# Attention, routed experts and an MLP in one kernel: routing the last batch in two groups, and moving weight loads, splits and slot loads around the first expert passes

## The chip, the cores and the metric

One core of a Trainium2 chip runs the whole program. The metric is device microseconds of one execution, lower is better. Engines are named as in the profile: PE (TensorE), DVE (VectorE), ACT (ScalarE), POOL (GpSimd), SP (SyncE, which here only issues DMAs; its queue is shown as SPq).

## What is computed

```python
# q, k, v: (4, 8, 576, 64)   s: (4, 8, 576)
scores = scale * q @ k.T                                   # causal
scores += min(-(cum[:, None] - cum[None, :]), 0)           # cum = cumsum(max(s, 0))
x = softmax(scores) @ v            # as 2304 tokens x 512
e = argmax(x @ w_gate, axis=1)     # 8 experts, one for each token
g = softmax(x @ w_gate)[e]
y[t] = g[t] * relu(x[t] @ w1[e]) @ w2[e]                   # w1 512x1024, w2 1024x512
h = y @ w_in                                               # 512x2048, float64 in DRAM
out = (h * clip(h + 3, 0, 6) / 6) @ w_out                  # 2048x512, float64 in DRAM
```

## The kernel before

**Precision.** Every product is taken with numbers split in two 16-bit halves, "hi" and "lo", and three matmuls stand for one. So each weight has to be loaded in float32 (64 pieces `wf` of 512 KB) and split. `piece` (lines 215 to 243) returns a job in two steps: `ld` takes a staging tile and issues the load on SP, `sp` splits it. With `act=True` the split is one ACT instruction (line 234) and one DVE instruction (line 237); with `act=2` it is POOL (229), ACT (230) and POOL (231).

**Attention.** A unit is 128 query rows (the fifth of a batch has 64) of one of the four batches: 20 units of 4 head pairs each, so N = 80 pairs. Line 973 walks the pairs; `todo` holds work for given slots n (`at_slot`), and `at_time` turns a time, counted with the prices of line 862, into a slot. The last two units are taken in the order 19, 18 (line 71).

**Routing.** For a finished unit `rows_out` scales the rows (ACT 639, POOL 640) and writes them to DRAM, `logits` transposes them by DMA and returns the gate's matmuls as `mm`. `route` (14 DVE instructions and one of ACT) picks the experts of a group of units, `place_tokens` ranks the tokens with small matmuls and scatters them into the slot table `tok_d` with one indirect DMA of POOL for each unit (line 739). `counts` (line 752) works out the tables of all passes after the last group; its result `dyn_i` is read by SP into registers. Before the change a batch is one group. Units 17, 19 and 18 are finished too late for the attention loop: their `mm`, then `route`, `place_tokens` and `counts` of the fourth batch, are hooks that run behind the blocks f = 0, 1, 2 and 4 of the first expert pass.

**Expert passes.** There are ten passes over `CAP_A`, 128 or `CAPS` rows. Passes 0 and 1 take 224 rows each of experts 0 and 1, and only tokens of the first three batches; passes 2 and 3 take what is left of those two experts (128 rows); passes 4 to 9 take the other six, sorted by load. A pass p has eight blocks `expert_hidden` (f = 0..7, 12 matmuls, ReLU on ACT line 1046, lo half on DVE line 1047) and four output blocks (d = 0..3, 24 matmuls at line 1151, then lines 1157 to 1159). All share five PSUM buffers (pool `pb`). `load_slots` reads the slots of a pass (line 193), `load_x` gathers its rows by an indirect DMA of POOL (line 200) and transposes them by DMA on SP (line 204); both stand behind the hidden blocks of the pass two before. `feed(x)`, called behind block f as x = f and behind block d as x = 8 + d, issues loads and splits of coming weights; `load` orders each load behind a marked transpose with `tc.issue_after`, and `split` can be told (`early`) not to wait for `mark["pos"]`.

**What sets the order.** The program text gives priorities; a scheduler with a simulated timeline then puts each engine's instructions in the order in which it takes them to be ready. On the chip every engine and the SP queue keep that order, whatever is late. An instruction that was written later can so stand in front of one written earlier.

**Weights before the change.** In attention, `w_load` takes four pieces of w1 and four of w2 of expert 0 and three of w1 of expert 1, at slots 52, 54 .. 72, each split three slots later; the staging tiles are the two buffers "q32" of the attention's own loads. The five pieces left of expert 1 are loaded in pass 0 at x = 0..4, behind `mark["x0"]`, the transpose of unit 17, and split at x = 5..9. Pass 1 loads four of expert p4, pass 2 loads four more and splits four at its output blocks, pass 3 splits four.

Of the kernel before, what the change touches and what calls it, by code (L numbers as in the profile page):

```python
# [8 lines left out]
F32 = mybir.dt.float32  # L9
F16 = mybir.dt.float16  # L10
BF16 = mybir.dt.bfloat16
I32 = mybir.dt.int32
# [15 lines left out]

LATE = 5


@with_exitstack
def kernel(
# [160 lines left out]

    def load_x(p):

        t = (rings["odd"] if p % 2 else rt).tile([128, 2 * KD, (CAP + 15) // 16 * 16], F16, tag="xsT", name="xsT", bufs=1)
        for x, (a, m) in enumerate(blocks((passes[p] + 15) // 16 * 16)):
            xg = row_tile([128, 2 * DM], F16, "xg")
            mark["pool"] = nc.gpsimd.indirect_dma_start(  # L200
                out=xg[:m], out_offset=None, in_=x_d[:min(col0[u] for u in late) if p < NS else NT, :],
                in_offset=Offset(ap=slots[:m, p, x, 0:1], axis=0),
            ).ins
            mark["xs", p] = nc.sync.dma_start_transpose(out=t[:, :, a:a + m], in_=xg[:m]).ins
        return t


# [9 lines left out]
    def piece(src, halves, sc, view, act=False):  # L217
# [3 lines left out]
        def ld():  # L221
            f = stage[0].tile([128, 1024], F32, tag=stage[1], name="wf")
            fv = view(f)
# [60 lines left out]
    with ExitStack() as at:  # L284
        ac = at.enter_context(tc.tile_pool(name="ac", bufs=1))
        a2 = at.enter_context(tc.tile_pool(name="a2", bufs=2))
        a3 = at.enter_context(tc.tile_pool(name="a3", bufs=3))
        stage.update({0: a2, 1: "q32"})
        psS = at.enter_context(tc.tile_pool(name="psS", bufs=3, space=PSUM))
# [359 lines left out]
        def logits(u, g):  # L649
# [13 lines left out]

            if place[u] == NU - 3:
                mark["x0"] = mark["x"]

            def half(t, c):
# [245 lines left out]
        for b in range(B):  # L913
            us = [u for u in range(NU) if units[u][0] == b]
            groups += [us] if b + 1 < B else [g for g in (us[:NCH - LATE], us[NCH - LATE:]) if g]
        routed = 0
        hooks = {}
        for us in groups:
# [9 lines left out]
            for g, u in enumerate(us):  # L928
                e0 = NP * place[u] + NP + 1
                at_slot(e0, lambda u=u: rows_out(u))  # L930
                at_slot(e0 + 1, lambda u=u, g=g, mms=mms: mms.update({u: logits(u, g)}))
                d = 14.0 if R[units[u][1]] == 128 else 8.0
                if us[-1] + 1 == min(late):
                    d = 14.0
                t = begins[min(N, e0 + 1)]
                if us[0] == min(late) and place[u] >= NU - 3:
                    hooks.setdefault(min(len(hooks), 4), []).append(lambda u=u, mms=mms: mms[u]())
                    continue
                at_time(t + d, lambda u=u, mms=mms: mms[u]())
                routed = max(routed, t + d + 1.0)  # L940
            if us[0] == min(late):
                hooks.setdefault(4, []).append(lambda us=us: route(us))
                hooks.setdefault(4, []).append(lambda us=us: (place_tokens(us), counts()))
                continue
# [6 lines left out]
        w1_rest = []  # L951
        WS, WD = 28, 2

        def w_load(x):
            if x == KD:
                w0.extend(w2_jobs(of(0), act=2))
                w0.extend(w1_jobs(of(1), "odd", True))
                w1_rest.append(w0.pop())
            splits[x] = w0[x]()

        for x in range(KD + KF // 2 + KE):
            at_slot(N - WS + WD * x, lambda x=x: w_load(x))
            at_slot(N - WS + 3 + WD * x, lambda x=x: splits[x]())

# [35 lines left out]
    def double_piece(src, hi, lo):  # L1000
# [4 lines left out]
        def ld():  # L1005
            d = stage[0].tile([128, 512, 2], I32, tag=stage[1], name="wd")
            nc.sync.dma_start(d, src)
# [52 lines left out]
    with ExitStack() as ex_:  # L1060
# [3 lines left out]

        stage.update({0: ex_.enter_context(tc.tile_pool(name="ste", bufs=5, reuse_waits="tile")), 1: "wf"})
        xs = {0: xs0[0], 1: load_x(1)}
        jobs, pend = [], []
        DOUBLES = {4: 3, 5: 3, 6: 3, 7: 2, 8: 2, 9: 3}
        for p, rows in enumerate(passes):
# [13 lines left out]
            def load(k):  # L1083
                for ld in jobs[:k]:
                    with tc.issue_after(mark["x0" if p == 0 else ("xs", 2 if p == 1 else 1)]):
                        pend.append(ld())
# [7 lines left out]
            def feed(x):  # L1094

                if p == 0:
                    load(x < KD + 1)
                    split(5 <= x < 6 + KD, True)
                elif p >= PF:
                    load(2 if x >= KF else 1 + x % 2)  # L1100
                    split(max(0, len(pend) - (8 if hooks else 4 if jobs else 0)))
                elif p == 1:
                    load(x < KD)
                elif p == NS:
                    split(x >= KF)
                    load(x >= KF)
                else:
                    split(x < KD)

            for f in range(KF):  # L1110
                expert_hidden(wt1, xsT, rows, hT, f)
                if f == 4:
# [6 lines left out]
                    g = held[:, :rows, 1].bitcast(F32)  # L1119
                if p == 0:  # L1120
                    for h in hooks.pop(f, []):
                        h()
                if p and f % 2 == 1:
# [5 lines left out]
                feed(f)  # L1129
            if p + 2 < NPASS:  # L1130
                load_slots(p + 2)
                xs[p + 2] = load_x(p + 2)
            if p == 1:
# [12 lines left out]
            for d in range(KD):  # L1146
# [12 lines left out]
                (nc.vector.tensor_tensor if p < PF else gtt)(out=lo, in0=y, in1=hi, op=ALU.subtract)  # L1159
                feed(KF + d)  # L1160


# [181 lines left out]
```

## Time and profile before

| | |
|---|---|
| three timed runs | 910.68, 916.42, 926.51 us; median 916.42 us |
| the profiled execution | 909.41 us; span of its instructions 907.7 us |
| busy, share of the span | PE 91%, DVE 54%, ACT 46%, POOL 27% |
| mean granted TensorE clock | 0.960 |

Attention ends at about 276 us of the span, the ten expert passes at about 522, the MLP at 907. A timeline row gives start, duration, engine, line, operation, out<-in and count; in brackets the idle time of the engine just before it, and what ended that. In the clock columns 1.0 is 2.4 GHz and 0.5 is 1.2 GHz.

### The profile page before, as it was taken

What the parts mean: (1) busy time and instruction counts of PE and PEld (TensorE: products, weight loads), DVE (VectorE), ACT (ScalarE), POOL (GpSimd) and SP (SyncE); (2) the same over time, 40 slices, a digit from 0 to 9 for tenths busy, and PEclk for the clock granted to TensorE, in tenths of its full rate; (3) what the DMA queues carried; (4) which work ended last, traced back from release to release, by engine and by line L of the source; (5) the groups of instructions that cost most, each with busy time, mean ns of one, the idle gap of its engine ahead of it and who ended that gap; (6) DMA issues with size and microseconds to landing.
All of it is one profiled execution on the core that took longest, in us unless ns stands there. A gap on an engine that the chain in (4) does not pass through costs nothing.

```text
span 907.7 us, 17239 instructions
## 1 busy us (share of the span) xinstructions
PE 825.3 (91%) x6610; PEld 505.0 (56%) x6610; DVE 492.5 (54%) x1283; ACT 413.6 (46%) x795; POOL 240.7 (27%) x288
## 2 busy tenths in 40 slices
PE   1988989889986897998999999999999999999994
PEld 0456656566656896666777844444444444457441
DVE  5565775876865546797885569990252045014000
ACT  3565865767764135565554357660252045014000
POOL 2176775756642223142331100000000000000000
PEclk9989989989988998999999999999999999999997
DMA  7999999997639169999884103320000000000000
GB/s 184 177 175 183 183 183 195 185 172 161 167 78 221 40 187 288 287 308 283 243 279 129 71 23 105 105 71 24 24 0 13 24 13 1 23 24 1 24 24 26
DMA packets 166832, 111.32 MB, mean 123 GB/s; under 512 B 126038, under 2 KB 142678, under 8 KB 166742
## 3 DMA queue, kind: packets, MB, share of 16 engines
q1 hardware_dynamic: 162950, 100.08, 46.8%
q0 software_dynamic: 3792, 10.06, 3.3%
q8 instruction: 54, 0.88, 0.4%
q14 instruction: 36, 0.29, 0.1%
HBM read 78.65 MB, written 9.66 MB: 97 GB/s over the span
## 4 chain that ended last, share of the span: by engine, by line
issue 43%; PE 11%; DMA 6%; DVE 4%; POOL 2%; ACT 1%; another core or an unknown queue 1%; SPq 1%; POOLq 0%; DVEq 0%; ACTq 0%
PE py L1151 6%; PE ph L1042 5%; DMA wf<-in_moe_w_dram 3%; DMA wd<-in_moe_w_in_dram 2%; POOL out_dram L1212 2%; DVE t L237 1%; DMA row_d<-tok_d 1%; DVE hT L1047 1%; ACT t L234 1%; DVE m L1019 0%; DVE m L1020 0%; SPq L1142 0%; DVE wi L1022 0%; POOL x2T L1159 0%
## 5 line engine op out<-in xcount | busy, mean ns | idle before, releaser
L1171 PE MATMUL ph<-x2T,wi 128*128 128x512 f16 (+1 forms) x960 | 187.4, 358 | 0.0
L1054 PE MATMUL py<-wo,gT 128*128 128x512 f16 x864 | 187.1, 379 | 0.0
L1171 PEld LDWEIGHTS <-wi 128*128 128x128 f16 x960 | 93.9, 98 | 92.8
L1054 PEld LDWEIGHTS <-gT 128*128 128x128 f16 x864 | 84.6, 98 | 101.7
L1042 PE MATMUL ph<-xsT,t 128*128 128x224 f16 (+7 forms) x960 | 114.9, 283 | 21.3 <-DVE hT L1047 19.7
L1177 DVE SCALAR_TENSOR_TENSOR t<-t,ph 128x512 f32<-128x512 f32 (+1 forms) x80 | 50.5, 632 | 141.3 <-ACT t L1176 141.3
L1042 PEld LDWEIGHTS <-t 128*128 128x128 f16 x960 | 89.3, 102 | 44.9 <-issue 22.7
L1212 POOL DMA_INDIRECT out_dram<-o,orows x18 | 17.7, 983 | 355.6 <-ACT o L1210 346.2
L1151 PE MATMUL py<-hT,t 128*128 128x224 f16 (+7 forms) x960 | 108.9, 274 | 1.9 <-DVE hT L1047 1.6
L1151 PEld LDWEIGHTS <-t 128*128 128x128 f16 x960 | 86.0, 99 | 22.7 <-issue 2.7
L575 ACT ACTIVATE hi<-pt 128x256 f16<-128x256 f32 (+3 forms) x144 | 64.3, 461 | 63.9 <-PE pt L553 54.0
L576 DVE SCALAR_TENSOR_TENSOR lo<-pt,hi 128x256 f16<-128x256 f32 (+3 forms) x144 | 72.8, 519 | 31.6 <-ACT hi L575 31.3
L237 DVE SCALAR_TENSOR_TENSOR t<-wf,t 128x1024 f16<-128x1024 f32 x56 | 68.0, 1228 | 32.3 <-ACT t L234 32.3
L1210 ACT ACTIVATE o<-py 128x512 f32<-128x512 f32 x18 | 10.7, 597 | 163.5 <-PE py L1054 163.5
L540 ACT ACTIVATE pp<-ne,nm 128x128 f32<-128x128 f32 (+4 forms) x144 | 76.7, 578 | 12.9 <-DVE nm L534 11.7
L234 ACT ACTIVATE t<-wf 128x1024 f16<-128x1024 f32 x56 | 58.0, 1052 | 46.1 <-DMA wf<-in_moe_w_dram 39.6
L553 PE MATMUL pt<-idf,pp 128*128 128x128 f32 (+1 forms) x400 | 75.1, 309 | 1.2 <-ACT pp L540 0.6
L534 DVE CUSTOM_DVE_ANT_0 ne<-sp,cp 128x128 f32<-128x128 f32 (+4 forms) x144 | 61.1, 454 | 20.4 <-PE sp L521 10.7
L510 PE MATMUL sp<-kT,qT 128*64 128x128 f16 (+3 forms) x256 | 45.6, 342 | 26.6 <-DMA kT<-k 19.5
L1178 ACT ACTIVATE gT<-t 128x512 f16<-128x512 f32 (+1 forms) x80 | 46.8, 586 | 50.0 <-DVE t L1177 50.0
L1179 DVE SCALAR_TENSOR_TENSOR gT<-t,gT 128x512 f16<-128x512 f32 (+1 forms) x80 | 51.0, 638 | 31.3 <-ACT gT L1178 29.7
L1176 ACT ACTIVATE t<-ph,three 128x512 f32<-128x512 f32 (+1 forms) x80 | 51.2, 642 | 32.1 <-PE ph L1171 32.1
(149 smaller groups left out, 1052.0 us busy)
## 6 DMA issues: line engine op xcount, KB each, us to landing
wf<-in_moe_w_dram SPq DMA_DIRECT2D x64, 512.0 KB
wd<-in_moe_w_in_dram SPq DMA_DIRECT2D x16, 512.0 KB
wd<-in_moe_w_out_dram SPq DMA_DIRECT2D x16, 512.0 KB
v<-in_v_dram SPq DMA_DIRECT2D x36, 128.0 KB
k<-in_k_dram SPq DMA_DIRECT2D x8, 512.0 KB
q<-in_q_dram SPq DMA_DIRECT2D x8, 512.0 KB
x_d<-xw SPq DMA_DIRECT2D x16, 256.0 KB
cp<-cum_d SPq DMA_DIRECT2D x6, 576.0 KB
```

The costliest lines, as they stand in the source:

```text
L234: nc.scalar.activation(hi, fv, AF.Copy, scale=sc)
L237: stt(out=lo, in0=fv, scalar=sc, in1=hi, op0=ALU.mult, op1=ALU.subtract)
L534: mark["dve"] = nc.vector.tensor_tensor_reduce(out=ne[:, a:z], in0=sp, in1=c[:, a:z], op0=ALU.add, op1=ALU.min, scale=-1.0 / SC, scalar=se ...
L540: mark["act"] = nc.scalar.activation(self.view(self.pp, e), self.view(self.ne, e), AF.Exp, bias=self.nm[:, e:e + 1], scale=-1.0).ins
L553: nc.tensor.transpose(dst, src, idf)
L575: nc.scalar.activation(hi, pt, AF.Copy, scale=SP)
L576: stt(out=lo, in0=pt, scalar=SP, in1=hi, op0=ALU.mult, op1=ALU.subtract)
L1042: mark["pe"] = nc.tensor.matmul(ph[:, :n], wt[c][:, a, cols], xT[:, KD * b_ + c, :n], start=(c == 0 and x == 0), stop=(c == KD - 1 and x = ...
L1054: nc.tensor.matmul(py[:n], hT[i_][:, f, a:a + n], wt[:, j_, f, :], start=(f == 0 and x == 0), stop=(f == nk - 1 and x == 2),)
L1151: nc.tensor.matmul(py[:, :rows], wt2[:, j_, f, cols], hT[i_][:, f, :rows], start=(f == 0 and x == 0), stop=(f == KF - 1 and x == 2),)
L1171: nc.tensor.matmul(ph[:, :n], wi[:, a, kk, fs], x2[:, KD * b_ + kk, :n], start=(kk == 0 and x == 0), stop=(kk == KD - 1 and x == 2),)
L1176: nc.scalar.activation(t, ph[:, :n], AF.Relu, bias=three, scale=SH)
```

## The change

The last batch is routed in two groups: units 15, 16, 17 inside the attention loop (their `mm` by time, at slots 72, 75 and 78; `route` at 78, `place_tokens` at 79), and units 18, 19 as hooks: `mm` of 19 at x = 2, `mm` of 18 and `route` at x = 4, `place_tokens` at x = 6, `counts` at x = 8, behind the first output block of pass 0. The hooks now run inside `feed`. Staging in attention takes "k32" and "q32" in turn, so four buffers. The four w1 pieces of expert 0 keep their slots 52 to 58; the seven pieces behind them go from slots 60, 62 .. 72 to 66, 67, 69, 70, 72, 73, 75, each split three slots later as before. In pass 0 the first load waits for the last transpose of routed rows (unit 18), the others for the transposes of pass 1's rows; four of the five splits go to x = 8..11 and the fifth to x = 0 of pass 1. Behind the first output block of pass 0 the slots of passes 2, 3 and 4 are loaded at once, and the rows of pass 2 gathered. Pass 1 gathers and transposes for pass 3, pass 2 only gathers for pass 4, whose transposes follow pass 2's output blocks. The splits of p4's pieces are two in pass 2 (x = 8, 10) and six in pass 3 (x = 0..3, 8, 10).

```diff
-    def load_x(p):
-
-        t = (rings["odd"] if p % 2 else rt).tile([128, 2 * KD, (CAP + 15) // 16 * 16], F16, tag="xsT", name="xsT", bufs=1)
+    def gather(p):
+
+        got = []
...
+            got.append((xg, a, m))
+        return got
+
+    def turn(p, got):
+
+        t = (rings["odd"] if p % 2 else rt).tile([128, 2 * KD, (CAP + 15) // 16 * 16], F16, tag="xsT", name="xsT", bufs=1)
+        for xg, a, m in got:
             mark["xs", p] = nc.sync.dma_start_transpose(out=t[:, :, a:a + m], in_=xg[:m]).ins
         return t
+
+    def load_x(p):
+        return turn(p, gather(p))
...
-            f = stage[0].tile([128, 1024], F32, tag=stage[1], name="wf")
+            stage[1].append(stage[1].pop(0))
+            f = stage[0].tile([128, 1024], F32, tag=stage[1][0], name="wf")
...
-        stage.update({0: a2, 1: "q32"})
+        stage.update({0: a2, 1: ["k32", "q32"]})
...
-            groups += [us] if b + 1 < B else [g for g in (us[:NCH - LATE], us[NCH - LATE:]) if g]
+            groups += [us] if b + 1 < B else [g for g in (us[:NCH - LATE], us[NCH - LATE:NCH - LAST], us[NCH - LAST:]) if g]
...
-                if us[0] == min(late) and place[u] >= NU - 3:
-                    hooks.setdefault(min(len(hooks), 4), []).append(lambda u=u, mms=mms: mms[u]())
+                if us[-1] == max(late):
+                    hooks.setdefault(4 if place[u] == NU - 1 else 2, []).append(lambda u=u, mms=mms: mms[u]())
                     continue
...
-            if us[0] == min(late):
-                hooks.setdefault(4, []).append(lambda us=us: route(us))
-                hooks.setdefault(4, []).append(lambda us=us: (place_tokens(us), counts()))
+            if us[-1] == max(late):
+                hooks[4].append(lambda us=us: route(us))
+                hooks[6] = [lambda us=us: place_tokens(us)]
+                hooks[KF] = [counts]
                 continue
...
-        WS, WD = 28, 2
...
-            at_slot(N - WS + WD * x, lambda x=x: w_load(x))
-            at_slot(N - WS + 3 + WD * x, lambda x=x: splits[x]())
+            n = N - 28 + 2 * x if x < KD else N - 14 + (x - KD) * 3 // 2
+            at_slot(n, lambda x=x: w_load(x))
+            at_slot(n + 3, lambda x=x: splits[x]())
...
-                    with tc.issue_after(mark["x0" if p == 0 else ("xs", 2 if p == 1 else 1)]):
+                    with tc.issue_after(mark["x" if p == 0 and len(jobs) > KD else ("xs", 2 if p == 1 else 1)]):
...
                     load(x < KD + 1)
-                    split(5 <= x < 6 + KD, True)
+                    split(x >= KF, True)
+                    for h in hooks.pop(x, []):
+                        h()
...
                 elif p == 1:
+                    split(x == 0, True)
                     load(x < KD)
                 elif p == NS:
-                    split(x >= KF)
+                    split(x in (KF, KF + 2))
                     load(x >= KF)
                 else:
-                    split(x < KD)
+                    split(x < 4 or x in (KF, KF + 2))
...
-            if p + 2 < NPASS:
+            if p >= PF - 1 and p + 2 < NPASS:
                 load_slots(p + 2)
-                xs[p + 2] = load_x(p + 2)
+            if p and p + 2 < NPASS:
+                got = gather(p + 2)
+                if p != NS:
+                    xs[p + 2] = turn(p + 2, got)
...
+                if p == 0 and d == 0:
+                    for x in range(2, PF + 1):
+                        load_slots(x)
+                    xs[2] = load_x(2)
+            if p == NS:
+                xs[p + 2] = turn(p + 2, got)
```

## Rows read from the trace of the kernel before

**Rows 1.** The page's slices of 22.7 us: busy tenths of PE, granted clock.

```profile
PE   1988989889986897998999999999999999999994
...
PEclk9989989989988998999999999999999999999997
```

**Rows 2.** Stretches: length, busy us (count) of PE, PEld, DVE, ACT, POOL, clock, DMA share, GB/s.

```profile
283.40:289.50 6.10, 0.02 (x1) 0.00 (x0) 2.77 (x4) 2.61 (x4) 0.00 (x0) 0.73 1.03 334
289.50:293.00 3.50, 3.47 (x19) 2.75 (x19) 2.28 (x4) 3.04 (x5) 0.00 (x0) 0.50 1.11 324
...
305.40:308.80 3.40, 0.01 (x1) 0.01 (x1) 0.78 (x8) 0.36 (x1) 1.01 (x2) 1.00 0.01 1
...
340.00:345.40 5.40, 4.10 (x68) 3.74 (x66) 3.58 (x8) 1.22 (x3) 0.88 (x3) 1.00 0.86 160
345.40:350.50 5.10, 0.02 (x1) 0.02 (x1) 1.50 (x3) 2.59 (x7) 0.00 (x0) 0.71 0.97 323
...
390.00:430.00 40.00, 35.56 (x249) 24.24 (x248) 31.56 (x47) 23.29 (x38) 13.72 (x17) 0.99 0.93 296
```

**Rows 3.** Timeline of PE from the first expert pass to the fourth.

```profile
289.53 4.12 PE L1042 MATMUL ph<-xsT,t 128*128 128x224 f16 x24 [6.11 <-DVE hT L1047]
...
308.79 9.87 PE L1042 MATMUL ph<-xsT,t 128*128 128x224 f16 x84 [3.44 <-DVE hT L1047]
318.50 9.36 PE L1151 MATMUL py<-hT,t 128*128 128x224 f16 x96
...
334.24 5.52 PE L1151 MATMUL py<-hT,t 128*128 128x128 f16 x96
...
350.48 2.72 PE L1042 MATMUL ph<-xsT,t 128*128 128x128 f16 x24 [5.11 <-DVE hT L1047]
```

**Rows 4.** Timeline of ACT over the same stretch.

```profile
277.76 0.34 ACT L1046 ACTIVATE hT<-ph 128x224 f16<-128x224 f32 x1
285.06 1.06 ACT L234 ACTIVATE t<-wf 128x1024 f16<-128x1024 f32 x1 [6.96 <-DMA wf<-in_moe_w_dram]
...
307.95 0.36 ACT L1046 ACTIVATE hT<-ph 128x224 f16<-128x224 f32 x1 [10.97 <-remote]
...
347.91 1.06 ACT L234 ACTIVATE t<-wf 128x1024 f16<-128x1024 f32 x1 [6.69 <-DMA wf<-in_moe_w_dram]
```

**Rows 5.** Timeline of the SP queue: each row's duration is the issuing time there.

```profile
243.02 8.57 SPq L224 DMA_DIRECT2D wf<-in_moe_w_dram  x3
260.31 2.88 SPq L193 DMA_DIRECT2D slots<-tok_d  x2
268.18 2.58 SPq L204 DMA_TRANSPOSE xsT<-xg  x2
...
271.44 1.30 SPq L656 DMA_TRANSPOSE xT<-xw  x1
...
279.77 3.44 SPq L224 DMA_DIRECT2D wf<-in_moe_w_dram  x5
...
283.81 5.74 SPq L656 DMA_TRANSPOSE xT<-xw  x1
289.65 4.67 SPq L204 DMA_TRANSPOSE xsT<-xg  x2
...
331.01 12.19 SPq L204 DMA_TRANSPOSE xsT<-xg  x4
```

**Rows 6.** Timeline of POOL around the routing of the third and the fourth batch.

```profile
245.17 2.13 POOL L231 TENSOR_TENSOR t<-wf,t 128x1024 f16<-128x1024 f32 x1 [1.17 <-ACT t L230]
...
256.34 0.93 POOL L739 DMA_INDIRECT tok_d<-what,pos_s  x1 [0.31 <-issue]
...
305.78 0.93 POOL L739 DMA_INDIRECT tok_d<-what,pos_s  x1 [0.31 <-issue]
```

**Rows 7.** Timeline of PE at the end of the third batch's scatters.

```profile
256.79 0.23 PE L609 MATMUL o<-v,hi 128*64 128x64 f16 x2 [0.23 <-issue]
256.84 0.21 PE L609 MATMUL o<-v,lo 128*64 128x65 f16 x2
258.23 0.27 PE L609 MATMUL o<-v,hi 128*64 128x65 f16 x4 [1.18 <-issue]
```

More of the change, by code (lines that the diff above doesn't have):

```diff
@@ L29 @@
 LATE = 5
+LAST = 2
 @with_exitstack
@@ L662, in logits @@
                     ).ins
-            if place[u] == NU - 3:
-                mark["x0"] = mark["x"]
             def half(t, c):
@@ L956, in w_load @@
                 w0.extend(w2_jobs(of(0), act=2))
-                w0.extend(w1_jobs(of(1), "odd", True))
-                w1_rest.append(w0.pop())
+                w1_rest.extend(w1_jobs(of(1), "odd", True))
+                w0.extend(w1_rest[:KE])
+                del w1_rest[:KE]
             splits[x] = w0[x]()
         for x in range(KD + KF // 2 + KE):
-            at_slot(N - WS + WD * x, lambda x=x: w_load(x))
-            at_slot(N - WS + 3 + WD * x, lambda x=x: splits[x]())
+            n = N - 28 + 2 * x if x < KD else N - 14 + (x - KD) * 3 // 2
+            at_slot(n, lambda x=x: w_load(x))
+            at_slot(n + 3, lambda x=x: splits[x]())
         for n in range(-1, N + 20):
@@ L1005, in ld @@
         def ld():
-            d = stage[0].tile([128, 512, 2], I32, tag=stage[1], name="wd")
+            d = stage[0].tile([128, 512, 2], I32, tag=stage[1][0], name="wd")
             nc.sync.dma_start(d, src)
@@ L1063 @@
         rings["odd"] = r1
-        stage.update({0: ex_.enter_context(tc.tile_pool(name="ste", bufs=5, reuse_waits="tile")), 1: "wf"})
+        stage.update({0: ex_.enter_context(tc.tile_pool(name="ste", bufs=5, reuse_waits="tile")), 1: ["wf"]})
         xs = {0: xs0[0], 1: load_x(1)}
@@ L1119 @@
                     g = held[:, :rows, 1].bitcast(F32)
-                if p == 0:
-                    for h in hooks.pop(f, []):
-                        h()
                 if p and f % 2 == 1:
```

## The prediction, made before the changed kernel was run

> **What bounds the kernel now.** I read the page's slices first. PE is at 8 or 9 tenths throughout, but for the ends and two slices at 6 and 7 tenths, the thirteenth and the sixteenth (272 to 295 and 340 to 363 us), and the granted clock is below 9 tenths there too [rows 1]. So PE sets the time, and the kernel can only gain where PE stands or runs at 1.2 GHz. Then I cut that region into stretches and went through the timelines of PE, ACT, SP and POOL for what stands at the head of each queue. Three places come out.
>
> Place A, pass 0: PE stands 6.1 us [rows 2, 3], because ACT has a weight split in front of the ReLUs and waits 6.96 us for its load [rows 4]. The reader should see that the ReLU of block 0 ran at 277.76, and the split, written behind block 5, comes next: the scheduler had pulled it forward. Five PSUM buffers fill, and PE stops. On SP five loads went ahead of the transposes of unit 18 and of pass 1's rows, which then took 5.74 and 4.67 us to issue [rows 5]; another transpose of unit rows took 1.30.
>
> Place B, between passes 0 and 1: PE stands 3.4 us [rows 2, 3]. ACT waits on something the view calls remote until 307.95 [rows 4]; the only thing running is the last of five scatters on POOL, 305.78 to 306.71 [rows 6].
>
> Place C, pass 3: PE stands 1.3 us in the 5.4 before 345.4 and then 5.1 us [rows 2, 3]. SP needed 12.19 us for four transposes [rows 5]; loads of p4's weights queued behind them, ACT stood 6.69 us in front of such a load's split [rows 4], and the ReLUs stood behind ACT.
>
> Each stop is followed by slow matmuls. After A the clock is 0.50 for 3.5 us [rows 2]: 24 matmuls took 4.12 us where 24 of the 96 in 9.36 us take 2.34 [rows 3], so 1.8 us more. After C 24 took 2.72 against 24/96 of 5.52 = 1.38 [rows 3], 1.3 more. After B I put the loss at 1.1, between nothing and A's 1.8. So A is worth 7.9 us, B 4.5, C 7.7; together 20.1, or 2.2%.
>
> **The change, part by part.**
>
> *Pass 0, transposes ahead of loads.* SP now issues unit 18's transpose (1.3 us instead of 5.74), one load, the two transposes for pass 1 (2.6 us, as 268.18 shows, instead of 4.67), then four loads. Before, five loads issued from 279.77 had landed by about 292.5, some 2.5 us each. In the new order load 1 leaves near 281, the transposes near 286 to 289 (they wait for their gathers), the other four loads from 289, landing about 291.5 to 299. Pass 0 without a stop would run its hidden blocks from 276.2 to 285.5 (96 matmuls, 9.3 us) and its output blocks to 294.8. Splits at output blocks come due at about 288, 290, 292.5 and 295, the fifth at 296: each within 3 us of its load. ACT can be 3 us late before five PSUM buffers of 1.2 us or more each are full. I take 7 of A's 7.9 as won; the bounds are 0 (splits pulled forward again) and 7.9.
>
> *Routing in two groups, `counts` at x = 8.* The added work is one more `route`, and the same 20 scatters in all. Its DVE instructions last 0.15 to 0.3 us and lie beside matmuls of the first blocks; I cost them at nothing, and at 3 us if DVE had no room. At B, what ended at 308 was PE's own last matmul of block 0, 2.5 us late while a scatter was issued. The same had happened at the third batch: PE stands for 0.23 and 1.18 us with no visible wait while the fifth scatter runs (256.34 to 257.27) [rows 6, 7]. If this belongs to scatters it moves with them, into pass 0, and may come twice, for three and for two. So B gains 4.5 at best, and loses 2.5 at worst. I take 1.5: the lag stays, but output rows no longer wait behind the tables at the pass change.
>
> The Trainium skill (SBUF — State Buffer, "Who interferes with whom") says that PE and ACT never wait for another engine's access; then the scatters would not be the cause, and the stop would have no reason to move with them. The rows do not agree with that in timing, though they show no mechanism. By the page B would stay at 4.5 wherever the scatters go, and the sum would be 1.5 us higher.
>
> *Three slots at once, pass 4's transposes later.* Slots of passes 2 to 4 are asked for near 291, not at pass ends. SP stands there until `counts` is through and the scatters have landed (the third batch: last scatter ends 257.27, slots issued 260.31 [rows 5, 6], so 3 us). Behind it on SP wait pass 2's transposes and p4's loads; pass 2 begins only near 313 (294.8 and two times 9.3), so nothing is late. p4's first loads go out near 300 into a stretch where DMA is idle. In pass 2 four loads need staging buffers (five in all), so the eighth waits for the third split, in pass 3; pass 4's three transposes stand behind it on SP. Passes 2 and 3 take 4 x 5.5 = 22 us of PE, pass 3 half of that. Transposes start about 3 us into pass 3 and need 3.9 us (3 x 1.3) to 9.1 us (3/4 of 12.19), and land 2 us on: 9 to 14 us into a pass of 11. So C's 7.7 go, and 0 to 3 us come back; I take 6 won, bounds 0 and 7.7.
>
> *Staging in attention, later slots for seven pieces.* Four buffers instead of two free SP sooner. But three pieces that SP issued at 243.02, ahead of the slot loads at 260.31, now belong to slots 72, 73, 75, behind the slot loads of slot 71 in the text, and their splits on ACT to slots 75, 76, 78, the last pairs of attention. Four POOL splits (over 2.13 us each [rows 6]) move toward the third batch's scatters. The logits of unit 17, transposed at 271.44, now stand in the loop at slot 78. Cost: up to 17 us (the rival below), or a gain of up to 1.4 if the gaps of [rows 7] close. I take 2 lost: the three splits' ACT work is 3 x 1.06 us, most of it in front of the last pairs. The other passes (4.4 us idle in 390 to 430 [rows 2]) keep their distance to their loads; I leave them.
>
> **Sum:** -7 - 1.5 - 6 + 2 = -12.5 us, 1.4%. Against the profiled execution, 909.41, that is 896.9. The timed runs lie 1 to 17 us above it. The two lower ones and the profiled one average 912.2, which gives 899.7; the median 916.42 gives 903.9. I forecast **901**.
>
> **Rivals.**
>
> 1. *The stall moves into the tail of attention (slower).* SP stands at the slot loads until the scatters have landed, and at pass 0's transposes until 270.8 (268.18 + 2.58 [rows 5]). If the scheduler keeps the three late loads behind both, they land near 273, 275.5 and 278, while ACT has their splits in front of the exponentials of the last pairs. For: the simulated order was about 7 us too early for loads at A. Against: it may see this wait and place the splits later. Price: the last four pairs begin about 264, at 3 us each before 276, so up to 278 - 264 = 14 us of tail, plus 3 for the clock, less the 12.5 + 2 of the rest: 909.4 + 17 - 14.5 = 912; on the scale of the forecast, 915. It decides once ACT stands over 14 us less the clock's 3, so from about 11 us on.
>
> 2. *Splits are pulled forward again.* Nothing holds the `early` splits back but their loads. If ACT gets one in front of hidden blocks again, A keeps its 7.9, and only C and B are won: 909.4 - 1.5 - 6 + 2 = 903.9; on the same scale 908. For: it is what rows 4 show. Against: loads now issue 9 us later, so the simulated readiness is later too.
>
> 3. *All three places go, and the tail is no worse:* 909.4 - 20 = 889, scale 893. Against: B's cause isn't seen, and pass 4's transposes stand behind a buffer wait.
>
> 4. *The order comes out nearly as before, so that the change hardly does what it says:* within 3 us of 912.
>
> **How the numbers follow.** Forecast 0.42, rival 1 0.18, rival 2 0.15, rival 3 0.17, rival 4 0.08. A measurement of this kernel can tell about 2% from no change, that is 18 us. Rival 3 and a quarter of the forecast's spread lie at or past that on the fast side; only rival 1 together with a lost clock or B twice reaches it on the slow one. Faster 0.27, same 0.65, slower 0.08. The range goes from rival 3 less the later passes' room to rival 1 and the timed runs' own spread: 887 to 917.
>
> **What would show it.** A right: in pass 0 no ACT wait for `wf` over 3 us, unit 18's transpose at about 1.3 us on SP, PE without a gap over 2 us between 276 and 305. B: a PE lag of 1 to 2.5 us at the last scatter of a group. C: slots of passes 2 to 4 issued together, no 5 us gap in pass 3, perhaps 0 to 3 us before pass 4. Tail: pass 0 begins within 3 us of 276. Wrong: a start of pass 0 past 281, or ACT standing over 5 us at line 234 anywhere before pass 4.

## The result, and the profile after

The change made the kernel slower, by less than the 2% that the forecast named. 20 timed runs of each gave a median of 922.85 us (912.28 to 929.78) after and 914.88 us (898.51 to 926.51) before, 8.0 us or 0.9% apart; the ratio is 1.0143, 95% interval 1.0096 to 1.0191. Every ratio here is taken over a kernel's fast runs alone, those within 1.5% of its fastest (14 of the 20 after, 6 of the 20 before), while the medians are of all runs, which is why the two don't divide out. A second series of the changed kernel, without any edit (e10 below), gave 1.0104, 1.0043 to 1.0165. The forecast was 901, in a range of 887 to 917.

Line numbers of the changed kernel are its own: 688 is the gates' matmul (677 before), 750 the scatter (739), 203 and 214 the gather and the transpose of a pass (200, 204), 1055 and 1167 the two matmuls of a pass (1042, 1151), 248 and 251 the split on ACT and DVE (234, 237). The variants' lines are shifted by a few more. In the kernel before, the pairs are walked from line 965, the order 19, 18 stands in line 76 and the slot prices in line 815.

The page's slices of the changed kernel, to be read against [rows 1]:

```profile
PE   1988989899894796999999999999999999999994
...
PEclk9987689896795998999999999999999999999998
```

The low slices are now the thirteenth and the fourteenth (4 and 7 tenths, 276 to 322 us), and the sixteenth is at 6 (7 before). The fourth and fifth, at a clock of 7 and 6, lie where the two programs have the same order on every engine. The windows of before and after for 60 to 120 us (columns as in [rows 2]) show that difference by itself, 0.91 against 0.69:

```profile
60.00:120.00 60.00, 54.49 (x698) 36.85 (x699) 39.84 (x153) 40.78 (x90) 45.50 (x55) 0.91 1.05 188
```

```profile
60.00:120.00 60.00, 55.64 (x594) 36.07 (x594) 31.67 (x122) 34.01 (x75) 40.24 (x50) 0.69 0.91 174
```

Long stretches at 1.2 GHz come in attention in some executions and not in others of the same order, so absolute times of two traces can't be compared; I compare distances between events.

PE's timeline after, from the end of attention to pass 3, answers to [rows 3]:

```profile
290.04 0.19 PE L688 MATMUL pl<-wg,xT 128*128 128x16 f16 x1 [10.72 <-DMA xT<-xw]
...
294.88 5.22 PE L1055 MATMUL ph<-xsT,t 128*128 128x224 f16 x36
...
308.26 0.18 PE L688 MATMUL pl<-wg,xT 128*128 128x16 f16 x1 [4.74 <-DMA xT<-xw]
...
322.41 9.36 PE L1055 MATMUL ph<-xsT,t 128*128 128x224 f16 x96
...
357.79 0.83 PE L1055 MATMUL ph<-xsT,t 128*128 128x128 f16 x12 [3.42 <-DVE y L1173]
359.33 1.19 PE L1055 MATMUL ph<-xsT,t 128*128 128x128 f16 x12 [0.71 <-DVE hT L1060]
365.22 1.01 PE L1055 MATMUL ph<-xsT,t 128*128 128x128 f16 x8 [4.70 <-DVE hT L1060]
```

A new stop of 10.72 us stands in the tail of attention, at the logits of unit 17. Place A's 6.11 us went, but 4.74 us came at the logits of unit 18. Place B's 3.44 us are gone. Place C has 3.42 + 0.71 + 4.70 = 8.8 us instead of 1.02 + 0.56 + 0.71 + 5.11 = 7.4.

Why the logits of unit 17 are late is read from POOL and SP (rows 5 and 6 of before show the same steps):

```profile
266.74 1.07 POOL L750 DMA_INDIRECT tok_d<-what,pos_s  x1 [15.75 <-DVE acc L760]
...
280.16 1.02 POOL L203 DMA_INDIRECT xg<-x_d,slots  x1 [7.28 <-issue]
281.49 0.94 POOL L203 DMA_INDIRECT xg<-x_d,slots  x1 [0.31 <-issue]
282.44 1.16 POOL L654 TENSOR_TENSOR xw<-xr,xw 128x512 f16<-128x512 f32 x1
```

```profile
275.64 0.90 SPq L196 DMA_DIRECT2D slots<-tok_d  x2
283.54 2.59 SPq L214 DMA_TRANSPOSE xsT<-xg  x2
...
286.85 1.30 SPq L670 DMA_TRANSPOSE xT<-xw  x1
...
302.57 1.52 SPq L670 DMA_TRANSPOSE xT<-xw  x1
...
305.97 3.46 SPq L214 DMA_TRANSPOSE xsT<-xg  x2
```

It is one chain over five queues: the third batch's scatters on POOL (from 266.74), its slots on SP, pass 0's two gathers on POOL, and behind them on POOL unit 17's low half (282.44); pass 0's two transposes on SP, and behind them unit 17's (286.85); then PE. The last pairs of attention stand on PE behind the logits that wait for all this.

And why the scatters are late is read from DVE, first before, then after (line 679, then 690, takes over a unit's logits; the rows of 64 partitions are the third batch's last, those ahead of them its last but one):

```profile
229.78 0.16 DVE L679 TENSOR_REDUCE lg<-pl 128x8 f32<-128x16 f32 x1
...
238.79 0.16 DVE L679 TENSOR_REDUCE lg<-pl 64x8 f32<-64x16 f32 x1
...
249.88 0.16 DVE L736 TENSOR_TENSOR pos_s<-rk,ps 128x5 int32<-128x5 f32 x1
...
250.04 1.19 DVE L237 SCALAR_TENSOR_TENSOR t<-wf,t 128x1024 f16<-128x1024 f32 x1
```

```profile
238.71 0.17 DVE L690 TENSOR_REDUCE lg<-pl 128x8 f32<-128x16 f32 x1
...
244.12 2.32 DVE L251 SCALAR_TENSOR_TENSOR t<-wf,t 128x1024 f16<-128x1024 f32 x1
...
248.76 1.22 DVE L251 SCALAR_TENSOR_TENSOR t<-wf,t 128x1024 f16<-128x1024 f32 x1
...
249.90 0.16 DVE L690 TENSOR_REDUCE lg<-pl 64x8 f32<-64x16 f32 x1
...
250.69 1.38 DVE L251 SCALAR_TENSOR_TENSOR t<-wf,t 128x1024 f16<-128x1024 f32 x1
...
266.31 0.15 DVE L747 TENSOR_TENSOR pos_s<-rk,ps 128x5 int32<-128x5 f32 x1
```

From the third batch's last logits to its slot numbers took 249.88 - 238.79 = 11.1 us, and now 16.4. Before, the splits of the second expert came behind the slot numbers; now all three stand ahead of them, and the routing's small steps are spread between more of attention's: 45 DVE instructions start in that stretch before, 62 after, and of the splits only the one of 1.38 us lies inside it. The other two lie ahead of the last logits, and those are late too: from the last but one to the last logits took 9.0 us before and 11.2 now. It is 11.2 to 11.5 us in the six traces that have the changed staging with its splits unheld, and 7.6 to 9.1 in the other eleven.

### The profile page after: what moved, and what is told of

It is laid out like the page before. It is cut to its first block, busy times and chain, and to the rows that moved or that the text cites. A ratio compares the mean times of both kernels' runs of the same rounds, so it can differ in the third digit from the quotient of the medians.

```text
span 921.1 us, 17231 instructions
## 1 busy us (share of the span) xinstructions
PE 836.0 (91%) x6604; PEld 510.3 (55%) x6604; DVE 497.6 (54%) x1302; ACT 414.7 (45%) x796; POOL 243.2 (26%) x288
## 4 chain that ended last, share of the span: by engine, by line
issue 45%; PE 8%; DMA 7%; POOL 3%; DVE 3%; SPq 1%; ACT 1%; POOLq 0%; DVEq 0%; ACTq 0%
PE py L1167 5%; DMA wf<-in_moe_w_dram 3%; PE ph L1055 3%; DMA wd<-in_moe_w_in_dram 2%; POOL out_dram L1234 2%; DVE t L251 1%; ACT t L248 1%; DMA xg<-x_d,slots 1%; DMA xT<-xw 1%; DVE wi L1035 1%; DVE hT L1060 0%; SPq L238 0%; POOL tok_d L750 0%; POOL x2T L1175 0%; DMA xsT<-xg 0%
## 5 line engine op out<-in xcount | busy, mean ns | idle before, releaser
L1232 ACT ACTIVATE o<-py 128x512 f32<-128x512 f32 x18 | 10.7, 597 | 163.6 <-PE py L1067 163.6
L567 PE MATMUL pt<-idf,pp 128*128 128x128 f32 (+1 forms) x400 | 79.9, 323 | 4.4 <-DVE lo L590 3.4
L554 ACT ACTIVATE pp<-ne,nm 128x128 f32<-128x128 f32 (+4 forms) x144 | 76.7, 578 | 13.0 <-DVE nm L548 11.5
L251 DVE SCALAR_TENSOR_TENSOR t<-wf,t 128x1024 f16<-128x1024 f32 x56 | 70.0, 1264 | 22.0 <-ACT t L248 21.7
L524 PE MATMUL sp<-kT,qT 128*64 128x128 f16 (+3 forms) x256 | 48.4, 369 | 25.8 <-DMA kT<-k 19.3
L623 PE MATMUL o<-v,hi 128*128 128x65 f16 (+2 forms) x960 | 62.1, 209 | 5.5 <-DVE xr L636 4.4
```

The costliest lines, as they stand in the source:

```text
L251: stt(out=lo, in0=fv, scalar=sc, in1=hi, op0=ALU.mult, op1=ALU.subtract)
L554: mark["act"] = nc.scalar.activation(self.view(self.pp, e), self.view(self.ne, e), AF.Exp, bias=self.nm[:, e:e + 1], scale=-1.0).ins
L567: nc.tensor.transpose(dst, src, idf)
L623: mark["pe"] = nc.tensor.matmul(dst, a, x, start=first, stop=last).ins
```

## The experiments

Three distances, each read from one trace, tell the variants apart. R: from the third batch's last logits to its slot numbers (both DVE rows above). T: from those logits to the first matmul of pass 0. P: from there to the end of the span. The changed kernel's two traces differ by 0.1, 0.8 and 0.3 us in them; R differs by 1.3 us between e14 and e16, which have the same edits up to there. T starts at the last logits and so leaves out that they come late themselves.

| kernel | R | T | P | median, us | ratio to before |
|---|---|---|---|---|---|
| before | 11.1 | 37.4 | 631.5 | 914.88 | |
| after | 16.4 | 45.0 | 626.2 | 922.85 | 1.0143 (1.0096 to 1.0191) |
| after, again | 16.5 | 45.8 | 625.9 | 921.27 | 1.0104 (1.0043 to 1.0165) |
| e1 unit 17 in pass 0 | 16.4 | 38.0 | 627.2 | 911.79 | 1.0014 (0.9974 to 1.0055) |
| e2 old staging | 11.1 | 40.2 | 622.0 | 915.54 | 0.9996 (0.9936 to 1.0057) |
| e3 before + staging | 16.5 | 38.2 | 630.3 | 913.21 | 1.0060 (1.0023 to 1.0096) |
| e4 before + groups | 11.1 | 41.0 | 626.6 | 912.19 | 1.0013 (0.9971 to 1.0056) |
| e8 splits behind | 9.5 | 41.6 | 628.5 | 911.20 | 1.0005 (0.9966 to 1.0044) |
| e14 tail mended | 9.5 | 37.0 | 625.4 | 906.98 | 0.9919 (0.9866 to 0.9973) |
| e15 passes alone | 11.0 | 36.1 | 632.3 | 908.60 | 1.0004 (0.9959 to 1.0048) |
| e5 before, registers | 11.1 | 36.5 | 628.2 | 908.24 | 0.9973 (0.9928 to 1.0018) |
| e6 after, registers | 16.3 | 44.1 | 620.1 | 911.33 | 1.0006 (0.9972 to 1.0039) |
| e7 all mended | 10.9 | 36.4 | 628.3 | 906.91 | 0.9948 (0.9907 to 0.9989) |
| e11 splits placed | 11.1 | 36.5 | 620.7 | 903.56 | 0.9854 (0.9805 to 0.9904) |
| e12 after, registers, splits | 16.3 | 45.7 | 620.4 | 922.21 | 1.0039 (0.9998 to 1.0081) |
| e13 splits last | 10.9 | 36.1 | 623.2 | 903.24 | 0.9923 (0.9883 to 0.9963) |
| e16 staging kept | 10.8 | 38.4 | 620.6 | 905.29 | 0.9881 (0.9799 to 0.9964) |

The median of the kernel before was 908.8 to 914.9 in these series; each ratio is to its own series.

**e1 to e4: which part makes the tail late.** My theory was the logits of unit 17, the rival the staging. e1 moves the logits and the first group's routing to pass 0:

```diff
+                if us[0] == min(late) and u == us[-1]:
+                    hooks.setdefault(0, []).append(lambda u=u, mms=mms: mms[u]())
+                    continue
                 at_time(t + d, lambda u=u, mms=mms: mms[u]())
...
+            if us[0] == min(late):
+                hooks[0].append(lambda us=us: route(us))
+                hooks[1] = [lambda us=us: place_tokens(us)]
+                continue
```

> The changed kernel, with the logits of unit 17, the routing and the placing of units 15 to 17 taken out of the attention loop and put behind hidden blocks 0 and 1 of pass 0. Theory 1 (the loss is PE standing 10.72 us at unit 17's logits in front of the last pairs): that stop goes, and 10 to 13 us with it, so about 911 us, ratio to the kernel before 0.99 to 1.00. Theory 2 (the loss comes from the staging part, which delays the third batch's routing): the stop shrinks but pass 0 still begins past 285 us, less than 4 us gained, 919 or more.

e2 undoes the staging part in the changed kernel, e3 adds it alone to the kernel before:

```diff
-        stage.update({0: a2, 1: ["k32", "q32"]})
+        stage.update({0: a2, 1: ["q32"]})
...
-            n = N - 28 + 2 * x if x < KD else N - 14 + (x - KD) * 3 // 2
+            n = N - 28 + 2 * x
```

> The changed kernel with the staging part undone: one staging tag with two buffers in attention, loads at the old slots. Theory 1: PE still stands about 8 to 11 us at unit 17's logits, time 920 to 925. Theory 2: the third batch's first scatter comes at 250 to 255 us instead of 266.74, the stop shrinks to under 4 us, and the time falls by 8 us or more, to 915 or less.

> The kernel before with the staging part alone (two tags in turn, later slots for seven pieces). Theory 1: within 3 us of the kernel before, no stop over 4 us in attention's tail. Theory 2: slower by 8 us or more, the third batch's first scatter at 260 us or later.

e4 gives the kernel before the two groups alone (`us[NCH - LATE:NCH - LAST], us[NCH - LAST:]`, and the hooks of units 19 and 18 as in the change, with `counts` at x = 7):

> The kernel before with the routing in two groups alone (units 15 to 17 in the loop, units 18 and 19 behind blocks 2 to 7 of pass 0, the tables behind block 7). Theory 1: PE stands 8 to 11 us at the logits of unit 17 in attention's tail; the stops in passes 0 and 3 remain, the one between passes 0 and 1 goes; slower than the kernel before by 4 to 9 us. Theory 2: no such stop over 4 us; 0 to 4 us faster than the kernel before.

PE's stops in the tail: e1, e3 and e4 (e2 has one of 4.92 us at unit 17's logits).

```profile
285.33 2.42 PE L1062 MATMUL ph<-xsT,t 128*128 128x224 f16 x12 [7.23 <-DMA xsT<-xg]
```

```profile
277.29 2.42 PE L1044 MATMUL ph<-xsT,t 128*128 128x224 f16 x12 [7.41 <-DMA xsT<-xg]
```

```profile
285.01 0.20 PE L678 MATMUL pl<-wg,xT 128*128 128x16 f16 x1 [4.84 <-DMA xT<-xw]
```

Neither theory alone holds. R goes with the staging: 16.4 to 16.5 in the three kernels that have it, 11.1 in the two that don't. With staging alone PE stands 7.4 us for pass 0's rows, but attention itself ended 277.29 - 7.41 - 239.07 = 30.8 us after those logits instead of 37.4, so T is only 0.8 longer (38.2); from the last but one logits to pass 0 it is 49.6 instead of 46.4, 3.2 longer, and e3's ratio is above 1. The groups alone put the logits in front of the last pairs: T 41.0, 3.6 longer. Both together: 45.0, 7.6 longer, because the logits wait behind a chain that the staging has made 5.3 longer. So e1, e2 and e4 came out within noise of the kernel before.

**e8 and e14: the splits on DVE, and the tail alone.** e8 holds the three splits back; e14 does that and e1's edit.

```diff
+        def late_split(x):
+            with tc.issue_after(mark["pos"]):
+                splits[x]()
...
-            at_slot(n + 3, lambda x=x: splits[x]())
+            at_slot(n + 3, lambda x=x: splits[x]() if x < KD + KF // 2 else late_split(x))
```

> The changed kernel; the splits of the three pieces of w1 of the second expert stand on DVE behind the third batch's slot numbers. Theory (these splits, pulled ahead by the added staging buffers, spread the routing steps on DVE): from the last logits of the third batch to its slot numbers 11 to 12.5 us instead of 16.4, the stop in attention's tail 5 to 7 us instead of 10.72, time 4 to 6 us below the changed kernel, 917 to 919. Rival (the routing is late for another reason): 15 us or more, time within 2 us of the changed kernel.

> The changed kernel with only its attention tail mended: unit 17's logits and the first group's routing behind blocks 0 and 1 of pass 0, and the three splits of the second expert behind the third batch's slot numbers. Theory (the loss sits in the tail, and these two edits are its two halves): PE stands 3 us or less at the end of attention instead of 10.72 or 12.1, pass 0 begins 88 to 91 us after the second batch's first scatter where no long stretch at 1.2 GHz falls in between; 7 to 11 us less than the changed kernel, ratio 0.998 to 1.003. Rival (something else of the staging part is late too): a stop of 5 us or more stays, ratio 1.005 or more.

PE's stop at unit 17 in e8, and the first matmul of pass 0 in e14:

```profile
280.59 0.19 PE L688 MATMUL pl<-wg,xT 128*128 128x16 f16 x1 [3.41 <-DMA xT<-xw]
```

```profile
276.74 1.31 PE L1066 MATMUL ph<-xsT,t 128*128 128x224 f16 x12
```

With the splits behind, R fell to 9.5 and the stop to 3.41, with four staging buffers still there: the routing was late through the splits that the staging let run ahead, and not through the added buffers. With both edits no stop over 2.1 us is left in the tail and T is 37.0. The kernel is then faster than before, and by more than e14's term foresaw (0.9919, expected 0.998 to 1.003).

**e10: the changed kernel again.** Four variants had come out at 1.00, so I measured it once more beside others.

> The changed kernel once more, unchanged. Four variants of it, each with one part undone or mended, came out at 0.9996 to 1.0014 of the kernel before. If each of those edits really won 10 to 13 us, the changed kernel is again 1.010 to 1.019 of the kernel before. Rival: part of the first ratio belongs to the runs, since the long stretches at 1.2 GHz near 80 us and 207 us, where the two programs have the same order, come in some executions only; then it is 1.000 to 1.008 now.

1.0104, with a stop of 12.10 us at unit 17 and of 5.04 at unit 18: the stops and a loss came again, so they are the kernel's. The interval (1.0043 to 1.0165) holds both the theory's 1.010 and the rival's 1.008, so the size is not settled. The expectation's premise of the same order holds near 80 us only: near 207 us the two programs differ already (ACT's order differs from 200 us on, PE's from 209).

**e15: the passes alone.** The changed kernel with e2's edit and one group (hooks as before):

> The changed kernel without the staging part and without the two groups: what is left is the order of transposes and loads in pass 0, the splits' new places and the slots of passes 2 to 4 asked for at once. By the forecast's terms for A and C this alone would win 7 + 6 us, ratio 0.984 to 0.988. By the runs so far (C is register loads and splits ahead of their loads, which these edits leave) only A can go: gaps of 5 us or more stay in passes 3 and 4, ratio 0.992 to 0.999; if A comes back as well, 1.000 or more.

By the stops the last alternative came; the interval of the ratio can't tell it from the one before. PE's rows in passes 0 and 3:

```profile
282.01 0.19 PE L688 MATMUL pl<-wg,xT 128*128 128x16 f16 x1 [5.63 <-DMA xT<-xw]
...
341.07 1.44 PE L1054 MATMUL ph<-xsT,t 128*128 128x128 f16 x12 [2.62 <-DVE y L1172]
347.08 4.00 PE L1054 MATMUL ph<-xsT,t 128*128 128x128 f16 x36 [4.57 <-DVE hT L1059]
```

P is 632.3, no better than before (631.5). Alone, the new order of loads, transposes and splits won nothing; the two groups alone reach 626.6 (e4), about what the change won behind attention (626.2). Whether the order is worth something beside the groups is not shown: e2, which has both and the old staging, reaches 622.0, but with a stop of 4.01 us at unit 18's logits and stops of 4.67 and 4.11 in pass 3, at a mean clock of 0.98 from pass 0 to the MLP where e4 had 0.96.

**e5 and e6: what stands in front of place C.** The row of 12.19 us in [rows 5] holds four transposes. The view by source line of the kernel before takes it apart (columns: count, shortest, median and longest in ns, first and last start):

```profile
L204 SPq DMA_TRANSPOSE xsT<-xg x4: 1232/1295/1318, 331.0 to 341.9; - x4
```

```profile
L170 SPq TENSOR_LOAD <-dyn_i x9: 267/270/683, 332.4 to 338.0; - x9
```

The four take 5.1 us. Between the first and the second stand nine register loads of `dyn_i` and one of `nblk`, from 332.4 to 339.1: about 0.6 us each with the two short instructions behind it. The scheduler had pulled the registers of passes 5 to 9 forward. e5 (kernel before) and e6 (changed) order them behind the weight loads ahead of them in the text:

```diff
-            nc.sync.dma_start(fv, src)
+            mark["wf"] = nc.sync.dma_start(fv, src).ins
...
+            with after(*(["wf"] if p > PF else [])):
                 regs[kind, p] = nc.values_load(
...
+        with after("wf"):
             stop = nc.values_load(nblk, min_val=0, max_val=NT // 128)
```

> The kernel before; the eleven register loads (places and ranks of passes 5 to 9, and the block count of the rest loop) are ordered on SP behind the weight loads that stand ahead of them in the text, so that none stands between the transposes of pass 4. Theory (stop C is the register loads on SP, 332.37 to 339.10, in front of three transposes and three weight loads): the gaps of PE in passes 3 and 4, 1.02 + 0.56 + 0.71 + 5.11 = 7.4 us, fall to 2.5 or less, and the time by 5 to 7 us, ratio 0.992 to 0.995. Rival (the transposes or a buffer are slow by themselves): those gaps stay at 5.5 us or more, time within 2 us.

> The changed kernel with the same eleven register loads ordered behind the weight loads. Theory: its gaps in passes 3 and 4, 3.42 + 0.71 + 4.70 = 8.8 us, fall to 3 or less; 5 to 7 us less than the changed kernel, 916 to 918, ratio to the kernel before 1.005 to 1.010. Rival: gaps at 6 or more, 921 or more.

Half true at best. The gaps fell from 7.4 to 0.82 + 0.41 + 0.54 + 0.94 + 0.71 + 2.69 = 6.1 in e5, which by its own terms is the rival's side (5.5 or more), and from 8.8 to 0.71 + 4.19 = 4.9 in e6, between the two; P fell by 3.3 and 6.1. In time e5's gain can't be told from none. So the register loads are a part of C and not the whole.

**e7, e11, e12, e13, e16: the rest of C, and the best kernel.** e7 joins the edits of e1, e2 and e6, takes the hooks of units 19 and 18 to x = 6 and 7, `place_tokens` to x = 8, and holds the splits of pass 0 behind its last ReLU (`with after("act")`):

> The changed kernel with the staging part undone, unit 17's logits and the first group's routing behind blocks 0 and 1 of pass 0, the logits of units 18 and 19 behind blocks 6 and 7, the second group's placing behind the first output block, the splits of pass 0 behind its last ReLU on ACT, and the register loads behind the weight loads. If the causes named so far are all there is: no stop over 2.5 us between 270 and 375 us, gaps there 5 us or less in all instead of 17 in the kernel before, 898 to 904 us, ratio 0.980 to 0.990. If stops only move (rival): another stop of 4 us or more in passes 0 to 2, ratio 0.995 or more.

T fell to 36.4, but a stop of 4.55 us in pass 0, now at the ranking of the second group's tokens, and stops of 1.64 + 0.71 + 4.35 in pass 3 are there: the rival's stop, and a ratio of 0.9948, between the two. e11 places the splits by what needs them:

```diff
-                    split(x >= KF, True)
+                    with after("act"):
+                        split(x in (KF + 1, KF + 3), True)
...
-                    split(x == 0, True)
+                    with after("act"):
+                        split(x < 3, True)
...
-                    split(x < 4 or x in (KF, KF + 2))
+                    with after("act"):
+                        split(x < 2 or x >= KF)
```

> The variant with everything mended, and the splits placed by what needs them: two pieces in the output blocks of pass 0, three in hidden blocks 0 to 2 of pass 1, two in hidden blocks of pass 3 and the last four in its output blocks, each behind the ReLU ahead of it on ACT. Theory (what is left of C, 1.64 + 0.71 + 4.35 us, and the 4.55 us in pass 0 are splits that stand in front of ReLUs or routing steps while their loads are late): both stops under 1.5 us, 6 to 9 us below the variant before, 898 to 902, ratio 0.985 to 0.990. Rival (the weight loads come late wherever the splits stand): a stop of 3 us or more at the output blocks of pass 1 or of pass 4, ratio 0.993 or more.

e12 is e6 with these places only:

> The changed kernel with the register loads behind the weight loads and the splits placed as in the run above; staging, unit 17's logits and the routing as changed. Theory: the stops of passes 0 (at the logits of unit 18) and of attention's tail stay, 4 and 8 to 11 us, the stops of passes 3 and 4 go; 4 us less than the changed kernel with the register loads alone, ratio 0.994 to 0.999. Rival: as above, ratio 1.001 or more.

PE of e11, passes 0 and 3:

```profile
307.58 0.17 PE L739 MATMUL pr<-oh,upper 128*128 128x8 f16 x1 [6.58 <-DVE oh L714]
...
350.19 0.83 PE L1062 MATMUL ph<-xsT,t 128*128 128x128 f16 x12 [1.21 <-DVE hT L1067]
351.52 0.83 PE L1062 MATMUL ph<-xsT,t 128*128 128x128 f16 x12 [0.50 <-DVE hT L1067]
```

As the theory had it, place C all but goes: with the registers and the splits moved it keeps 0.55 + 1.21 + 0.50 = 2.3 us, and e12 shows much the same (0.17 + 1.21 + 0.50). e12's P did not improve on e6's, since its stop at unit 18 grew from 4.31 to 6.60 us, and its tail kept 11.52: a miss, the rival's side, and the ratio of 1.0039 is that of a kernel with the tail as changed. e11's stop in pass 0 was a miss as well: 6.58 us where 1.5 were expected. Its ratio, 0.9854, is still the lowest of all.

e13 moves e11's two splits of pass 0 to its last output block, behind the routing on ACT and DVE (`split(2 * (x == KF + 3))`):

> The variant with the splits placed (903.56 us), with the two splits of pass 0 moved to its last output block, behind the second group's routing on ACT and DVE. Theory (its stop of 6.57 us at the second group's slot numbers comes from these splits standing in front of the routing steps while their loads are late): the stop goes to 1.5 us or less, 4 to 7 us less, 897 to 900, ratio 0.978 to 0.984. Rival (the loads themselves are late, and the first blocks of pass 1 wait instead): a stop of 3 us or more in the first 12 us of pass 1, ratio 0.985 or more.

```profile
308.35 1.21 PE L1062 MATMUL ph<-xsT,t 128*128 128x224 f16 x11 [2.95 <-DVE y L1183]
312.60 0.55 PE L1062 MATMUL ph<-xsT,t 128*128 128x224 f16 x2 [3.04 <-DVE t L252]
314.25 9.86 PE L1062 MATMUL ph<-xsT,t 128*128 128x224 f16 x72 [1.09 <-DVE y L1183]
```

The rival: the stop moved into pass 1 (7.1 us instead of 6.6). In e11 ACT waited 6.80 us for the load of such a split, in e13 4.03: the loads themselves are late there, and neither place of the splits mended it. e16 is e11 with e8's edit in place of e2's:

> The changed kernel with its tail mended as in the run before (staging part kept, three splits behind the third batch's slot numbers, unit 17 in pass 0) and passes 0 to 4 as in the variant with the splits placed (logits of units 18 and 19 later, splits placed, register loads behind the weight loads). Theory (tail and passes are separate, so the gains add): no stop over 3 us in attention's tail, none in passes 3 and 4, the one of 4 to 6.6 us in pass 0 stays; 896 to 902 us, ratio 0.982 to 0.990, 4 to 6 us less than with the tail mended alone. Rival (they overlap): within 2 us of the run with the tail alone mended, ratio 0.990 to 0.997.

0.9881, inside the theory's range, but the interval holds the rival's too; a stop of 4.62 us came in its tail, where the theory had none over 3. With the splits held back, the added buffers show no loss clear of the noise (e8, e14, e16).

## Why the prediction was wrong

**The sign.** The step that failed is the last part of the change, "I take 2 lost". It named the logits of unit 17, "now stand in the loop at slot 78" (79 by the slot prices), and gave them no price, though [rows 5] had what was needed: their transpose at 271.44 stands on SP behind pass 0's two at 268.18. In the kernel before nobody on PE waited for it until pass 0. T grew by 7.6 us where 2 were forecast; e1, with these logits in pass 0, has it at 38.0, and e14, with the splits held too, at 37.0. Both signs of being wrong that the prediction named came: pass 0 began past 281, and ACT stood over 5 us at a split. Rival 1 had the place and about the size (11 us decide; the stop is 10.72) but not the mechanism: the three splits ran on ACT at 243.02, 245.72 and 248.05, earlier than before, not late. They hurt on DVE, where an order that has them ahead of the routing stretches it: held behind the slot numbers (e8), R fell from 16.4 to 9.5. "I cost them at nothing", said of the second `route`, asked only where DVE has room in pass 0; the third batch's routing in the loop was not looked at.

**A, 7 forecast.** 6.11 us went and 4.74 came: 1.4 by the gaps. ACT still waited 6.18 us for a split's load, which is rival 2's condition:

```profile
309.42 1.06 ACT L248 ACTIVATE t<-wf 128x1024 f16<-128x1024 f32 x1 [6.18 <-DMA wf<-in_moe_w_dram]
```

And the term asked only for ACT; that PE itself would stand at unit 18's logits for their transpose was not in it. The order on SP did come out as forecast (unit 18's transpose in 1.52 us), but it was issued only at 302.57, at the end of the same late chain. e15, without that chain, shows 5.63 at the same place. So the gain failed by itself.

**B, 1.5 forecast, 0 to 4.5 open.** All 3.44 us went. The next rows are POOL's last two scatters after:

```profile
319.18 1.00 POOL L750 DMA_INDIRECT tok_d<-what,pos_s  x1 [15.52 <-DVE n L773]
320.49 0.94 POOL L750 DMA_INDIRECT tok_d<-what,pos_s  x1 [0.30 <-issue]
```

PE has no gap beside them, nor beside the three at 294.82 to 298.43. The stop did not move with the scatters, as I had supposed against the Trainium skill (SBUF — State Buffer, "Who interferes with whom"); these rows agree with the page. The forecast had also read [rows 7] too far: the wait of 1.18 us began at 257.05 and lasted to 258.23, mostly after that scatter's end at 257.27. What the stop was stays open: 3.0 to 3.3 us in e5 and e15 with one group, 0.9 in e3, twice 0.9 in e4. In each of the three traces that have it, ACT's ReLU waits right there for what the view calls remote (10.97 us before, 11.07 in e5, 3.95 in e15); no other trace has such a row at the start of pass 1.

**C, 6 forecast.** 1.4 us were lost. The failed step is the reading "SP needed 12.19 us for four transposes": the row's length held ten register loads. Moving the transposes moved the registers with them (eleven, 347.6 to 353.3, ahead of the transposes at 353.95), and the split on ACT that waited 6.69 us waits 9.46 now:

```profile
362.65 1.06 ACT L248 ACTIVATE t<-wf 128x1024 f16<-128x1024 f32 x1 [9.46 <-DMA wf<-in_moe_w_dram]
```

e6 moves the registers (4.9 us of gaps left), e12 the splits as well (1.9 left).

**The sum.** T + 7.6 and P - 5.3 make 2.3 us, or 4.5 counted from the last but one logits, since the last came 2.2 later; the medians differ by 8.0 and 6.7. In the two traces the rest lies before those logits, where the mean clock of 200 to 240 us was 0.79 in the changed kernel's trace and 0.99 in the one of before. In e4's it was 0.66, though its order leaves that of before only with a memset at 251.45, so such a stretch needs no change of the program; whether the changed kernel meets them more often was not settled, and with it where the remaining 3.5 us of the medians' 8.0 come from (1.4 of 6.7 in the second series).

## What to carry to other kernels

When work moves into a stage, follow its whole chain through every in-order queue and ask what stands behind it there: one matmul of 0.2 us held the last pairs for 10.7. More buffers let work run ahead, also ahead of the small steps that a critical chain needs; order it behind them, which took the chain here from 16.4 us to 9.5. And take a timeline row that groups several instructions apart by source line before giving its length to them.

## What the runs showed of the hardware

Register loads are not free on the queue that issues DMAs: 0.27 us for the load and about 0.6 with its short followers, in order, so ten held SP for 6.7 us. The Trainium skill (DMA: Bandwidth & Descriptors, "Latency and other measured facts") gives a floor of about 600 ns for a `tensor_load`; the load by itself lies below that here, at 0.27, and only with its followers does it come to about 0.6. And the granted clock differed between executions where the order was the same (0.69 against 0.91 for 60 to 120 us, above): the first scatter of the first batch came at 124.17 us in one profile and at 136.80 in the other.
